# A fused attention and gated-MLP kernel on one core: the whole instruction order replaced, wv loaded ahead of the gate weights

## The chip, the cores and the metric

The kernel runs on one core of a Trainium2 chip. The metric is the device time of one execution in microseconds; lower is better. A core has a matrix engine (TensorE, PE in the profile; its weight loads are PEld), a vector engine (VectorE, DVE), an activation engine (ScalarE, ACT), a general engine (GpSimd, POOL) and a queue engine (SyncE, SP) that here does nothing but issue DMA transfers. Every engine works through its own list of instructions in order; between engines there are semaphores.

## The reference

Two branches read the same x (2048 tokens of 512 numbers, bf16) and are mixed by a gate per token. Branch A is attention with a compressive memory over 4 segments of 512 tokens, 32 heads of 16; branch B is a gated MLP with 1792 hidden features.

```python
g = sigmoid((x * gate_w).sum(-1, keepdims=True))
# A: q, k, v = x @ wq, x @ wk, x @ wv, in 32 heads of 16 and 4 segments of 512 tokens
for s in range(4):
    p = softmax(qs @ ks.T * scale + causal mask)
    a_dot = p @ vs
    a_mem = (phi(qs) @ M) / (phi(qs) @ z + 1e-6)      # phi(t) = t + 1 if t > 0 else exp(t)
    o = sigmoid(beta) * a_mem + (1 - sigmoid(beta)) * a_dot
    M, z = M + phi(ks).T @ vs, z + phi(ks).sum()
a = o @ wo
# B
b = (relu(x @ W_gate) * (x @ W_up)) @ W_down
out = g * a + (1 - g) * b
```

## The kernel before

All weights and the work of one segment lie in SBUF. `program` lists every operation of the whole computation once (1515 of them), each with what it reads and writes, and nothing in that list says when it runs. `Sched` then takes, for each of the five engines, a list of operation numbers from the table `ORDER`, walks the five lists and puts in the waits that the reads and writes call for. So the table alone decides in which order the engines work, and for a few operations which engine does them: the ReLU, the copies of q, k and v out of PSUM, the masking of k (`kp`) and the scaling of the output tile may stand in ACT's list or in DVE's. A second table, `BANKS`, gives for each accumulation the PSUM bank, of which there are eight; a matmul that begins in a bank waits until the engine that emptied it last is done. The tables were found by a search off the chip, with a planner's durations for each operation and with landing times for the first loads (`LAND0`, `DCOST`).

What PE does, by line of the code:
- L508: matmuls of ones at the start, of no use to the result. L520, L529: the first 512 tokens of x, loaded as hT, are transposed into xT by the identity; DVE and ACT copy the result (L513). Later chunks of x come transposed by DMA (L456).
- L591, L589: projections. q and k are made with features on the partitions (L591, weights wq, wk as the stationary side), v with tokens on the partitions (L589, wv as the moving side, so each of its matmuls needs one piece of wv whole: two matmuls in one operation take pieces 0 and 1, the next operation 2 and 3). The first segment's q is made in single steps, the first one in 384 and 128 columns.
- L706: attention scores, in visits of four to fourteen matmuls that use 32 rows of the array each. ACT turns them into exponentials (L717) and POOL zeroes the masked part (L726).
- L756: probabilities times values, 64 matmuls for each group of 8 heads, from vaug and from vsh, a copy of vaug shifted by 64 partitions that a DMA makes (L667). A column of vaug (L537, `vone`) makes the softmax's sums. DVE transposes, divides and transposes back (L764 to L779).
- L631, L648: the memory M and the read from it.
- L844: gate and up matmuls (wg, wu); ReLU (L852 on ACT, L853 on DVE), then the product with up (L855 on DVE) into hT.
- L881, L874: the output, seven pairs of matmuls over the hidden features (wd) and four over the heads (wo) into one bank; then a scaling by 1 - g into osb (L889 on DVE, L890 on ACT) and a store (L892). The last tile is made in two pieces of 384 and 128 columns.

Loads are issued on SP, but for hT2 (256 KB, 256 tokens of x), the first piece of wq and three tiny ones, which ACT issues (L452 for all). Each weight comes in pieces: wq, wk, wv in four of 128 KB, wg and wu in eight of 224 KB, wd in seven of 256 KB. gwb is the gate's weight spread over the partitions. ACT also loads its table at the first activation (L461).

The score visits, the L756 groups and the full matmuls differ in the part of the array they use.

Of the kernel before, what the change touches and what calls it, by code (L numbers as in the profile page):

```python
# [26 lines left out]
BANKS = ("171630520531275446756000000000047560000111115764767560667657445465554456464777507755157600774404414613500240251657751003"  # L27
         "423366410145546576053600571667673176267001021605702356603331563046063015614701000001404666454577127755074066545726565745"
         "67451706507275244216302403520425407020000014023307526164674767547654471210567123")
ORDER = {k: [int(x) for x in v.split()] for k, v in {  # L30
    "pe": """
# [17 lines left out]
1506 1481 1490 1500 1472 1482 1501 1491 1492 1502 1507 1508 1509 1510 1511 1512""",  # L49
    "act": """  # L50
# [5 lines left out]
1362 133 1326 1300 1473 1483 1493 1503""",  # L56
    "dve": """
# [9 lines left out]
1317 1463 1457 134 1464 1318 1458 1374 1366 1367 1368 1375 1376 1369 1370 1377 1371 1378 1372 1379 1380 1513""",  # L67
    "pool": """
# [331 lines left out]
def build_kernel(nc, A_x, A_wq, A_wk, A_wv, A_wo, A_beta, W_g, W_u, W_d, gate_w, out):  # L400
# [4 lines left out]
    EPS, SCALE = 1e-6, 16 ** -0.5  # L405
    sc = Sched(ORDER, BANKS)
    T = {}
# [539 lines left out]
```

## Time and profile before

| | us |
|---|---|
| median of 3 runs | 265.52 |
| the runs | 263.29, 265.52, 265.70 |
| the profiled execution | 263.63 |
| its span, first to last instruction | 262.4 |
| PE busy | 258.1 |
| ACT busy | 186.7 |
| DVE busy | 171.8 |
| POOL busy | 120.5 |

The profile shows one execution. A row of a group has the line of the code, engine and operation, what is written and read (`out<-in`), the shape, the number; then the total busy time in us and the mean of one in ns; then the idle time of the engine ahead of it and what ended most of that. A row of the order in time begins with the start in us and the length of the (merged) group; a bracket at its end tells how long the engine was idle ahead and for whom. `PEq`, `SPq`, `ACTq` are the queues that issue instructions. The records of matmuls overlap: a matmul of 512 columns is on record for 0.38 us, while the next one may start 0.216 us after it.

### The profile page before, as it was taken

Reading aid. Unit: us, or ns where it says so; the run is one execution under the profiler, and the core shown is the slowest. Engines: PE = TensorE matmul, PEld = TensorE weight load, DVE = VectorE, ACT = ScalarE, POOL = GpSimd, SP = SyncE. Lnnn points to the kernel's source line nnn. Section 1 sums busy time; section 2 is a strip of 40 time slices with the busy share of each in tenths; the row PEclk is TensorE's granted clock in tenths of the full one; section 3 lists DMA queues with packets and bytes.
Section 4 is the critical chain, followed back from the end, with each engine's and each line's share of the span. In section 5 each row is a group of like instructions: output and inputs, shape, how many; then the busy total and the mean of one; then the engine's idle time right before and its main releaser. Section 6 shows DMA issues by size and latency. Waiting matters only on the chain.

```text
span 262.4 us, 6451 instructions
## 1 busy us (share of the span) xinstructions
PE 258.1 (98%) x2655; PEld 116.4 (44%) x2655; DVE 171.8 (65%) x348; ACT 186.7 (71%) x179; POOL 120.5 (46%) x295
## 2 busy tenths in 40 slices
PE   8999999999999999999999999999999999999997
PEld 5333434444544445434544444444444445433553
DVE  2366777868867657987666716887766248866670
ACT  4579877877678855889666788887878855887103
POOL 2000586787052492466740458418734781148300
PEclk9999999999999999999999999999999999999999
DMA  7999984004205141030270300221030305200002
GB/s 213 263 307 203 298 170 140 25 3 120 45 3 124 27 117 23 2 80 1 63 128 20 81 4 0 80 45 40 2 65 1 83 3 83 42 2 0 2 2 80
DMA packets 34925, 19.61 MB, mean 75 GB/s; under 512 B 24144, under 2 KB 34256, under 8 KB 34896
## 3 DMA queue, kind: packets, MB, share of 16 engines
q1 hardware_dynamic: 34512, 18.80, 30.2%
q8 instruction: 21, 0.34, 0.6%
q10 hardware_dynamic: 384, 0.40, 0.5%
q14 instruction: 8, 0.07, 0.1%
HBM read 10.14 MB, written 2.11 MB: 47 GB/s over the span
## 4 chain that ended last, share of the span: by engine, by line
PE 94%; SPq 2%; DMA 2%; DVE 0%; issue 0%
PE ps L844 38%; PE ps L881 19%; PE ps L591 9%; PE ps L706 9%; PE ps L756 7%; PE ps L589 5%; PE ps L874 5%; SPq L452 2%; DMA wv<-in_A_wv_dram 2%; PE ps L648 1%; PE ps L631 1%; DVE rl L853 0%; DVE osb L889 0%
## 5 line engine op out<-in xcount | busy, mean ns | idle before, releaser
L717 ACT ACTIVATE E<-ps 128x2048 bf16<-128x2048 f32 (+2 forms) x87 | 135.3, 1582 | 32.8 <-PE ps L706 32.3
L726 POOL TENSOR_SCALAR_AFFINE_SELECT E<-E 64x256 bf16<-64x256 bf16 (+1 forms) x256 | 99.6, 419 | 100.2 <-ACT E L717 89.8
L844 PE MATMUL ps<-xT,wu 128*128 128x512 bf16 x224 | 60.5, 380 | 0.2 <-DVE rl L853 0.2
L844 PE MATMUL ps<-xT,wg 128*128 128x512 bf16 x224 | 59.9, 380 | 0.0
L881 PE MATMUL ps<-wd,hT 128*128 128x512 bf16 (+2 forms) x238 | 56.2, 367 | 0.0
L855 DVE TENSOR_TENSOR hT<-ps,rl 128x512 bf16<-128x512 f32 x56 | 38.1, 687 | 22.8 <-PE ps L844 22.3
L881 PEld LDWEIGHTS ps<-wd,hT 128*128 128x128 bf16 x238 | 21.4, 98 | 24.8 <-issue 2.8
L844 PEld LDWEIGHTS ps<-xT,wg 128*128 128x128 bf16 x224 | 20.6, 98 | 24.9 <-issue 1.9
L844 PEld LDWEIGHTS ps<-xT,wu 128*128 128x128 bf16 x224 | 19.9, 98 | 25.8 <-issue 3.4
L706 PE MATMUL ps<-qT,kp 32*128 32x320 bf16 (+7 forms) x512 | 27.6, 286 | 0.0
L853 DVE TENSOR_SCALAR rl<-ps 128x512 bf16<-128x512 f32 x28 | 19.2, 685 | 10.9 <-PE ps L844 10.7
L764 DVE STREAM_TRANSPOSE Tn<-ps 128x512 f32<-128x512 f32 x32 | 20.9, 693 | 6.4 <-PE ps L756 6.3
L852 ACT ACTIVATE rl<-ps 128x512 bf16<-128x512 f32 x28 | 16.5, 596 | 9.8 <-PE ps L844 9.8
L773 POOL TENSOR_TENSOR adT<-Tn,rdg 128x512 bf16<-128x512 f32 x12 | 13.1, 1095 | 20.4 <-DVE rdg L771 8.8
L706 PEld LDWEIGHTS ps<-qT,kp 32*128 32x128 bf16 x512 | 9.1, 92 | 24.2 <-ACT E L717 8.1
L589 PE MATMUL ps<-wv,xT 128*128 128x512 bf16 x64 | 17.4, 380 | 1.1 <-DMA wv<-in_A_wv_dram 1.1
L756 PE MATMUL ps<-E,vaug 64*17 64x128 bf16 (+7 forms) x512 | 18.2, 283 | 0.0
L756 PE MATMUL ps<-E,vsh 64*17 64x128 bf16 (+7 forms) x512 | 17.8, 283 | 0.0
L591 PE MATMUL ps<-xT,wk 128*128 128x512 bf16 x64 | 17.8, 380 | 0.0
L591 PE MATMUL ps<-xT,wq 128*128 128x512 bf16 (+2 forms) x68 | 17.6, 377 | 0.0
L889 DVE TENSOR_SCALAR osb<-ps,omg 128x512 bf16<-128x512 f32 (+1 forms) x10 | 7.1, 710 | 15.6 <-PE ps L874 15.6
L890 ACT ACTIVATE osb<-ps,omg 128x512 bf16<-128x512 f32 (+1 forms) x7 | 4.7, 672 | 16.5 <-PE ps L874 16.0
(70 smaller groups left out, 230.7 us busy)
## 6 DMA issues: line engine op xcount, KB each, us to landing
vsh<-vaug SPq DMA_DIRECT2D x8, 272.0 KB, 3.3
out_dram<-osb SPq DMA_DIRECT2D x15, 128.0 KB, 1.9
wg<-in_B_W_gate_dram SPq DMA_DIRECT2D x8, 224.0 KB, 5.5
wu<-in_B_W_up_dram SPq DMA_DIRECT2D x8, 224.0 KB, 5.6
osb<-in_A_x_dram SPq DMA_DIRECT2D x14, 128.0 KB, 2.2
wd<-in_B_W_down_dram SPq DMA_DIRECT2D x7, 256.0 KB, 3.6
wk<-in_A_wk_dram SPq DMA_DIRECT2D x4, 128.0 KB, 3.3
wv<-in_A_wv_dram SPq DMA_DIRECT2D x4, 128.0 KB, 3.7
```

The lines of the kernel that those rows point to most:

```text
L589: ins = e.matmul(A(ep)[:, :], lhsT=V.xT[:, kt, tok + col * 128:tok + (col + 1) * 128], rhs=w[:, kt, :], start=(kt == 0), stop=(kt == KT - 1))
L591: ins = e.matmul(A(ep)[:, c0:c1], lhsT=w[:, kt, col * 128:(col + 1) * 128], rhs=V.xT[:, kt, tok + c0:tok + c1], start=(kt == 0 and c0 == 0 ...
L706: ins = q.matmul(PS[:, ep.bank + i, o:o + w], lhsT=V.kp[r, kslot(s, G), c, :], rhs=V.qT[r, qslot(s, G), q0:q0 + w], start=True, stop=True, ...
L717: return a.activation(V.E[:, n * 512:(n + k) * 512].rearrange("q (b n) -> q b n", n=512), PS[:, x.bank:x.bank + k, :], ACT.Exp, scale=SCALE)
L726: pool(lambda g, ap=ap, lim=lim: g.affine_select(out=ap, in_=ap, compare_op=ALU.is_ge, fill=0.0, base=lim, pattern=[[0, 4], [1, 64]], chan ...
L756: ins = q.matmul(A(eps[p])[32 * jj:32 * jj + 17, 64 * (c + u):64 * (c + u + n)], lhsT=v[:, 8 * G + 2 * jj + p, :], rhs=V.E[r, f:f + 64 * n ...
L764: dve(lambda e, p=p, ep=eps[p]: e.transpose(V.Tn[:, 2 * (G % (TNN // 2)) + p, :], A(ep)[:, :]), 709, writes=[f"Tn{2 * (G % (TNN // 2)) + p ...
L844: ins = e.matmul(A(ep)[:, :], lhsT=w[:, kt, f * 128:(f + 1) * 128], rhs=V.xT[:, kt, c % XR * 512:(c % XR + 1) * 512], start=(kt == 0), sto ...
L852: sc.add(Op([("act", lambda e, ep=eg, r=r: e.activation(V.rl[:, r, :], A(ep)[:, :], ACT.Relu), t_act(512)), ("dve", lambda e, ep=eg, r=r: ...
L853: ("dve", lambda e, ep=eg, r=r: e.tensor_scalar(V.rl[:, r, :], A(ep)[:, :], 0.0, None, ALU.max), t_dve(512))],
L855: dve(lambda e, ep=eu, r=r, hs=hs: e.tensor_tensor(V.hT[:, hs, :], A(ep)[:, :], V.rl[:, r, :], ALU.mult), t_dve(512), reads=[f"rl{r}"], wr ...
L881: ins = e.matmul(A(ep)[:, 0:c1 - c0], lhsT=V.hT[:, slots[f], i * 128:(i + 1) * 128], rhs=V.wd[:, f, c0:c1], start=st_ and f == f0, stop=sp ...
```

## The change

The tables `ORDER` and `BANKS` are replaced; no other line differs, and the operations are the same ones. Two lines of each show the kind of edit:

```diff
     "act": """
-6 7 3 68 76 70 80 0 1 2 142 153 180 156 159 204 199 234 395 389 210 401 196 216 202 228 81 93 222 186 240 327 246 252 419 256 280 286 331 292 332
...
+3 6 7 68 70 76 80 0 1 2 153 142 145 156 169 159 204 193 234 389 210 199 216 401 228 93 81 407 222 240 186 246 419 252 256 449 280 286 335 292 336
...
     "sp": """
-4 5 8 9 10 11 12 13 14 15 17 18 27 20 19 16 24 21 22 90 26 23 39 25 32 88 31 38 50 28 40 98 163 37 30 29 162 35 49 33 47 34 96 45 36 208 207 44 42
...
+4 5 8 9 10 11 12 13 14 15 16 17 18 27 20 19 21 24 22 23 90 26 39 25 88 32 28 31 38 50 40 98 163 37 30 29 162 47 43 35 33 42 100 34 36 208 96 46 207
```

Operations 15 to 18 are the four pieces of wv, 19 to 26 the first halves of wg and wu, 27 is gwb; on ACT 3 is the table load with its first activation, 6 the load of hT2 and 7 that of wq. All five lists differ nearly everywhere behind the start. PE has 685 rows of equal instructions in place of 704. ACT does more of the work that either engine can do: ReLUs 31 in place of 28, copies of q 9 for 8, of k 6 for 4, of v 7 for 9, maskings of k 13 for 9, scalings of the output 8 for 6.

First place, the start. SP's loads of weights, before:

```order
L452 DMA wk<-in_A_wk_dram 128x512 x4
L452 DMA wv<-in_A_wv_dram 128x512 x3
L452 DMA gwb<-in_gate_w_dram 128x512
L452 DMA wg<-in_B_W_gate_dram 128x896 x2
L452 DMA wv<-in_A_wv_dram 128x512
L452 DMA wu<-in_B_W_up_dram 128x896
L452 DMA wg<-in_B_W_gate_dram 128x896 x2
```

and now:

```order
L452 DMA wk<-in_A_wk_dram 128x512 x4
L452 DMA wv<-in_A_wv_dram 128x512 x4
L452 DMA gwb<-in_gate_w_dram 128x512
L452 DMA wg<-in_B_W_gate_dram 128x896 x3
L452 DMA wu<-in_B_W_up_dram 128x896
L452 DMA wg<-in_B_W_gate_dram 128x896
L452 DMA wu<-in_B_W_up_dram 128x896
```

The fourth issued piece of wv moves up past gwb and two pieces of wg. PE at the same time, from the end of wq on, before:

```order
L591 MATMUL ps<-xT,wk 128x512 x2
L591 MATMUL ps<-xT,wq 128x512
L591 MATMUL ps<-xT,wk 128x512 x10
L591 MATMUL ps<-xT,wq 128x512
L706 MATMUL ps<-qT,kp 128x512 x4
L589 MATMUL ps<-wv,xT 128x512 x2
L591 MATMUL ps<-xT,wk 128x512 x2
L589 MATMUL ps<-wv,xT 128x512 x6
L844 MATMUL ps<-xT,wg 128x512 x2
```

and now:

```order
L591 MATMUL ps<-xT,wq 128x512 x12
L591 MATMUL ps<-xT,wk 128x512 x8
L589 MATMUL ps<-wv,xT 128x512 x2
L591 MATMUL ps<-xT,wk 128x512 x2
L589 MATMUL ps<-wv,xT 128x512 x2
L591 MATMUL ps<-xT,wk 128x512 x4
L706 MATMUL ps<-qT,kp 128x512 x4
L591 MATMUL ps<-xT,wk 128x512 x2
L589 MATMUL ps<-wv,xT 128x512 x6
L844 MATMUL ps<-xT,wg 128x512 x2
```

Value matmuls now begin ahead of the first scores. Second place, PE where the third segment's first output tiles are made (two tiles' worth of L874, four matmuls each; in brackets the semaphores that a row waits for), before:

```order
L874 MATMUL ps<-wo,oT 128x512 [waits s_dve]
L874 MATMUL ps<-wo,oT 128x512 x7
L844 MATMUL ps<-xT,wg 128x512 [waits s_act]
L844 MATMUL ps<-xT,wg 128x512 x3
L706 MATMUL ps<-qT,kp 128x256 [waits s_dve]
L706 MATMUL ps<-qT,kp 128x256 x7
L706 MATMUL ps<-qT,kp 128x320 [waits s_act,s_dve]
L706 MATMUL ps<-qT,kp 128x448 x2
L706 MATMUL ps<-qT,kp 128x192
L706 MATMUL ps<-qT,kp 128x64 x2
L844 MATMUL ps<-xT,wu 128x512 [waits s_dve]
L844 MATMUL ps<-xT,wu 128x512 x3
```

and now:

```order
L874 MATMUL ps<-wo,oT 128x512 [waits s_dve]
L874 MATMUL ps<-wo,oT 128x512 x7
L706 MATMUL ps<-qT,kp 128x256 [waits s_dve,s_act]
L706 MATMUL ps<-qT,kp 128x256 x7
L706 MATMUL ps<-qT,kp 128x320
L706 MATMUL ps<-qT,kp 128x448 x2
L706 MATMUL ps<-qT,kp 128x192
L706 MATMUL ps<-qT,kp 128x64 x2
L881 MATMUL ps<-wd,hT 128x512 [waits s_dve]
L881 MATMUL ps<-wd,hT 128x512 x3
```

The gate matmuls between the output and the scores are gone, and a further output tile begins right behind the scores; its wait for DVE is for L889 of the second tile. Third place, PE's end, before:

```order
L874 MATMUL ps<-wo,oT 128x512 x7
L881 MATMUL ps<-wd,hT 128x384 x2
L881 MATMUL ps<-wd,hT 128x512 x2
L874 MATMUL ps<-wo,oT 128x512 x4
L874 MATMUL ps<-wo,oT 128x384 x4
L881 MATMUL ps<-wd,hT 128x128 x10
L874 MATMUL ps<-wo,oT 128x128 x4
```

and now:

```order
L874 MATMUL ps<-wo,oT 128x512 x7
L881 MATMUL ps<-wd,hT 128x384 x2
L874 MATMUL ps<-wo,oT 128x512 x4
L881 MATMUL ps<-wd,hT 128x128 x2
L874 MATMUL ps<-wo,oT 128x128 x4
L881 MATMUL ps<-wd,hT 128x384 x2
L874 MATMUL ps<-wo,oT 128x384 x4
```

The two pieces of the last tile change places, so that the wider one is finished last; its scaling stands in ACT's list, that of the narrow one in DVE's.

More of the change, by code (lines that the diff above doesn't have):

```diff
@@ L26 @@
 CORDER = [[(0, 1, 7, 2, 6, 3, 5, 4), (4, 1, 7, 2, 6, 3, 5, 0)] * 2] * 4
-BANKS = ("171630520531275446756000000000047560000111115764767560667657445465554456464777507755157600774404414613500240251657751003"
-         "423366410145546576053600571667673176267001021605702356603331563046063015614701000001404666454577127755074066545726565745"
-         "67451706507275244216302403520425407020000014023307526164674767547654471210567123")
+BANKS = ("701342567041527367060111111000076674000000017746406641677557057660745455757454564555067547054561100243156300254312024440"
+         "000032601066124506725713302304356764655776571765057551202160263063036006466400000011667175542704477063043464664775757676"
+         "57661705075020500150260213503516547013213213546076745462767225760667057651602741")
 ORDER = {k: [int(x) for x in v.split()] for k, v in {
     "pe": """
[17 rows of a table removed]
-1506 1481 1490 1500 1472 1482 1501 1491 1492 1502 1507 1508 1509 1510 1511 1512""",
-    "act": """
[5 rows of a table removed]
-1362 133 1326 1300 1473 1483 1493 1503""",
-    "dve": """
[9 rows of a table removed]
-1317 1463 1457 134 1464 1318 1458 1374 1366 1367 1368 1375 1376 1369 1370 1377 1371 1378 1372 1379 1380 1513""",
-    "pool": """
[8 rows of a table removed]
-1364 1322 1358 1346 1329 1327 1340 1330 1360 1301 1302 1328 1324""",
[17 rows of a table added]
+1508 1509 1510 1471 1498 1481 1499 1472 1492 1500 1482 1511 1512 1501 1502""",
+    "act": """
[5 rows of a table added]
+1320 1344 1415 1332 1421 1350 1338 1439 1356 1433 1362 1326 1300 1457 1473 1503""",
+    "dve": """
[9 rows of a table added]
+1318 1368 1376 1369 1377 1370 1371 1372 1378 1379 1380 1493 1483 1513""",
+    "pool": """
[8 rows of a table added]
+1354 1358 1322 1352 1363 1327 1329 1364 1348 1328 1330 1301 1302""",
     "sp": """
[3 rows of a table removed]
-1484 1494 1504 1514""",
[3 rows of a table added]
+1494 1484 1514 1504""",
 }.items()}
```

80 rows, old and new, of the table ORDER are left out of this document.

## The prediction

> **What bounds the kernel now.** I read the page first, then the waits of TensorE (PE), then the start, the places of the waits and the end in order of time. From the page:
>
> ```profile
> span 262.4 us, 6451 instructions
> PE 258.1 (98%) x2655; PEld 116.4 (44%) x2655; DVE 171.8 (65%) x348; ACT 186.7 (71%) x179; POOL 120.5 (46%) x295
> ...
> PE 94%; SPq 2%; DMA 2%; DVE 0%; issue 0%
> ```
>
> PE (the first column of the busy line) is busy for 98% of the span and carries 94% of the chain that ended last. A new order can then win only three things: time in which PE stands still, the price of switching between kinds of matmul, and the two ends of the program. The longest of PE's waits (total us, times, longest):
>
> ```profile
> PE ps L589 <- DMA wv<-in_A_wv_dram: 1.1, 1, 1.1
> ...
> PE ps L844 <- DVE rl L853: 0.2, 1, 0.2
> ```
>
> One wait stands out, the one for a piece of wv. (The line left out is the launch, which no order moves.) Busy time alone hides part of a wait, because a matmul's record overlaps the next one's; so I take the pace of the starts as the measure. In the first fence below are pieces of the chain (start, length, what, how many), in the second rows in order of time:
>
> ```profile
> 72.72 0.55 PE ps L706 x14
> 94.14 2.59 PE ps L844 x12
> 186.12 1.10 PE ps L756 x64
> 128.50 2.14 PE ps L756 x127
> ```
>
> ```profile
> 24.48 0.59 PE L844 MATMUL ps<-xT,wu 128*128 128x512 bf16 x2
> 25.01 0.40 PE L706 MATMUL ps<-qT,kp 32*128 32x256 bf16 x8
> 25.34 0.60 PE L844 MATMUL ps<-xT,wu 128*128 128x512 bf16 x2
> ```
>
> Twelve full matmuls take 2.59 us, 0.216 each. After the two that start at 24.48 the next would start at 24.91; the scores start at 25.01, so leaving the full matmuls costs 0.10. Eight score matmuls (the step at L706) then hold PE for 0.33, fourteen for 0.55. Two neighbouring groups of L756 take 2.14 together, two lone ones 2 x 1.10, so putting them side by side saves 0.06.
>
> **The wait for wv (removed).** The start in order of time:
>
> ```profile
> 0.80 0.40 ACTq L452 DMA_DIRECT2D hT<-in_A_x_dram  x1
> 1.74 1.28 ACT L461 ACT_TABLE_LOAD   x1 [1.74 <-PEq L932]
> 3.03 0.21 ACT L461 ACTIVATE eb<-const-bfloat16-1.0 128x8 f32<-128x8 bf16 x1
> 4.13 0.85 PE L529 MATMUL ps<-ident,hT 128*128 128x128 bf16 x6
> 5.04 1.38 SPq L452 DMA_DIRECT2D wv<-in_A_wv_dram  x3
> 5.97 0.38 ACT L513 ACTIVATE xT<-ps 128x256 bf16<-128x256 f32 x1 [0.36 <-PE ps L529]
> 5.98 0.37 ACTq L452 DMA_DIRECT2D adT<-in_B_W_gate_dram  x1
> 7.89 0.43 SPq L452 DMA_DIRECT2D wv<-in_A_wv_dram  x1
> ...
> 12.14 0.40 PE L706 MATMUL ps<-qT,kp 32*128 32x512 bf16 x4
> 13.67 0.60 PE L589 MATMUL ps<-wv,xT 128*128 128x512 bf16 x2 [1.13 <-DMA wv<-in_A_wv_dram]
> ```
>
> Four score matmuls from 12.14 would hand over at about 12.14 + 0.33 = 12.47; the value matmuls start at 13.67. The wait costs 1.20 us. Its cause is the place of one 128 KB load on SP, issued at 7.89 behind gwb and two wg pieces:
>
> ```profile
> DMA to landing us min/median/max: 3.1/3.7/5.7
> ...
> hT<-in_A_x_dram ACTq DMA_DIRECT2D x1, 256.0 KB, 3.0
> out_dram<-osb SPq DMA_DIRECT2D x1, 96.0 KB, 1.6
> out_dram<-osb SPq DMA_DIRECT2D x1, 32.0 KB, 1.4
> ```
>
> (first row: the four pieces of wv). In the new order all four are issued one after another, so the fourth at about 5.04 + 3 x 0.475 = 6.5. With the median of 3.7 it lands at 10.2, with the worst of 5.7 at 12.2. In the old order the scores at 12.14 stand behind the transposes of x, 20 matmuls of wq and 12 of wk. In the new one the second pair of wv, the first to need the last two pieces, stands behind the transposes and as many matmuls: 20 of wq, 10 of wk, 2 of wv. So PE comes to it at 12.14 less the switch, 12.0, and to the first pair four matmuls earlier, at 11.2. At the median the wait is gone with 1.8 to spare, at the worst 0.2 is left: -1.20, bounds -1.20 and -1.0. The two wg pieces that stood ahead of that wv piece now stand behind it. They land about when it did, at 7.89 + 5.7 = 13.6, and their first matmul comes 14 matmuls and one visit of scores behind that pair, at 12.0 + 3.0 + 0.4 = 15.4. I cost this at nothing; what hides it is that margin of 1.8.
>
> **The small waits of the old order (-0.51).** Two more places are off the pace:
>
> ```profile
> 104.83 0.60 PE L844 MATMUL ps<-xT,wg 128*128 128x512 bf16 x2
> 105.46 0.43 PE L648 MATMUL ps<-Mbd,phiq 128*128 128x136 bf16 x4
> 143.15 1.03 PE L874 MATMUL ps<-wo,oT 128*128 128x512 bf16 x4
> 144.22 0.75 DVE L889 TENSOR_SCALAR osb<-ps,omg 128x512 bf16<-128x512 f32 x1 [0.28 <-PE ps L874]
> 144.97 0.62 PE L706 MATMUL ps<-qT,kp 32*128 32x256 bf16 x14
> 145.83 1.04 PE L844 MATMUL ps<-xT,wu 128*128 128x512 bf16 x4 [0.24 <-DVE rl L853]
> ```
>
> 104.83 + 2 x 0.216 = 105.26, but L648 starts at 105.46: 0.20, with no record of what it waited for. 144.97 + 0.55 = 145.52, but L844 starts at 145.83: 0.31, behind the ReLU on DVE. Both places are written anew, so both terms go.
>
> **A new wait at the third segment's boundary (+0.35).** In the new order the eight L874 matmuls are followed at once by the 14 score matmuls and then by L881 that waits for DVE: for the scaling at L889 of the tile that L874 has just finished. By the rows above: the last of four L874 starts at 143.80, DVE begins at 144.22, 0.42 later, and takes 0.75. With 0.05 for the signal (an estimate: 144.22 less 143.15 + 1.03, the end of the group) L881 is free 1.22 after the start of that matmul. PE gets there at pace after 0.216 + 0.10 + 0.55 = 0.87. So it waits 0.35; bounds 0 (if DVE's part is one of two waits and the other scaling, on ACT, is what it needs) and 0.75, a whole scaling.
>
> **Switches and groups (-0.26).** Full matmuls are left 61 times instead of 63: 2 x 0.10. The groups of L756 stand in 11 stretches instead of 12: 0.06. The number of matmuls of each kind is the same.
>
> **The end (+0.42).** The last tile's two column pieces change places: the 384 columns come last and go to ACT, where the 128 came last and went to DVE.
>
> ```profile
> L890 ACT ACTIVATE osb<-ps,omg 128x384 bf16<-128x384 f32 x1 | 0.6, 581 | 0.0
> L889 DVE TENSOR_SCALAR osb<-ps,omg 128x128 bf16<-128x128 f32 x1 | 0.3, 350 | 6.2 <-PE ps L874 6.2
> ```
>
> The scaling grows by 0.581 - 0.350 = 0.23, the store from 1.4 to 1.6 (its rows are above), 0.19 unrounded. Nothing lies beside them. 0 to 0.5.
>
> **Work moved from DVE to ACT (0).** By the counts of the two orders ACT gains 3 ReLUs, 3 copies of q or k, 4 maskings of k and 2 scalings, and loses 2 copies of v.
>
> ```profile
> L852 ACT ACTIVATE rl<-ps 128x512 bf16<-128x512 f32 x28 | 16.5, 596 | 9.8 <-PE ps L844 9.8
> L611 ACT ACTIVATE kp<-kT,pm 128x512 bf16<-128x512 bf16 x9 | 6.4, 716 | 0.0
> 150.00:247.00 97.00, 97.00 (x1081) 43.18 (x1087) 61.95 (x123) 73.10 (x67) 52.89 (x128) 1.00 0.15 31
> ```
>
> Taking a copy for as long as a ReLU, that is 4 x 0.596 net, 4 x 0.716, and 2 scalings at DVE's 0.75: 6.8 us. Between 150 and 247 us, in the last row, ACT is busy for 73.1 (the figure with x67) of 97: 24 us of idle in two fifths of the program cover it. Without that cover 6.8 is the upper bound; nothing on the path is the lower, and I take it, since a moved piece only costs where an exponential queues behind it.
>
> **Sum.** -1.20 - 0.51 - 0.26 + 0.35 + 0.42 = -1.2 us. The profiled execution took 263.63 us (its span and 1.2 around it), so one like it would take 262.4. It is 1.9 below the median of the three runs (263.29, 265.52, 265.70); the mean of all four is 264.5. I set the change on that mean: 263.3 us.
>
> [...]
>
> **Rivals.**
> *The table load holds hT back.* ACT now begins with the table load and its activation, ahead of the loads of hT (256 KB) and wq. If ACT issued them only when both are done, hT would be issued at 0.80 + 1.28 + 0.21 = 2.3 instead of 0.80, land 3.0 later at 5.3, and PE, which needs it at 4.13, would stand for 1.2: 263.6 like the profiled, 264.5 on the mean. Against it: at 5.98 ACT issues a load 0.01 after it began a copy of 0.38, so an issue does not wait for the work ahead. It costs something from a delay of 0.3 on.
> [...]
> *ACT becomes the bound, and the kernel slower.* Should 1.2 of the moved 6.8 us fall where the exponentials already hold PE, the gain is gone; with all of it the time is 263.3 + 6.8 = 270.1, and with 4.9 (268.2 less 263.3) it is over 1% slower than the median. For it: PE has no slack to give, and every score visit waits for an exponential. Against it: the idle time above.
> *The change does not take the wait away.* The value matmuls need their bank freed by a copy of q on ACT too. If that copy is what ends last, the 1.2 stays in another name: 264.5. Against it: the first pair comes 8 matmuls, 1.7 us, behind the last of wq, and a copy takes 0.6.
> *A late load elsewhere.* The shifted copy vsh is issued behind the ones column of v, which stands later in the new DVE order.
>
> ```profile
> 28.94 1.17 SPq L667 DMA_DIRECT2D vsh<-vaug  x2
> 40.21 1.10 PE ps L756 x64
> DMA to landing us min/median/max: 2.9/3.3/6.9
> ```
>
> Its halves are issued at 28.94 and 29.5; with the worst 6.9 the second is there at 36.4, 3.8 us ahead of the first L756. The new DVE order has the ones column behind the second chunk's first copy of k; I put that 3 us later, and SP has a wd piece between the halves: second half near 33. With 6.9 it lands at 39.9, against a first L756 1.2 earlier than before, at 39.0: 0.9 lost, 264.2. With the median 3.3 it has 2.7 to spare.
>
> **How the numbers follow.** The sum as worked out: 0.66, 263.3. Table load 0.07, 264.5. Wait kept under another name 0.07, 264.5. Late loads 0.12, 264.2. ACT bound 0.08, 264.5 to 270.1, over 1% slower for the last third. One per cent of 265.52 is what a measurement of this kernel can tell from no change, so faster means under 262.9. The runs reach 1.2 to either side of their mean; a median of three lies nearer. Of the first case I take 0.4 below 262.9, which gives 0.26; slower (over 268.2) gets 0.06: 0.03 of ACT's case, and 0.03 for what I did not see; within 1% 0.68. The range: down to 261.7, where the new waits come to nothing (0.35 and 0.42 less) and the runs are low; up to 265.7, which takes in all rivals but ACT's far end.
>
> **What would show it.** No wait of PE for wv at 11 to 14 us; PE's first L529 still at 4.1 and ACT's issue of hT at 0.8 (right) or 2.3 (table load); a wait of 0.35 at L881 behind L889 near 143; L890 with 384 columns as the last instruction, the end 0.4 later after PE's last matmul. Wrong would be a PE whose waits add up to over 1.5 us, or a row of L717 ahead of PE's waits in many places.

## The result and the profile after

| | before | after |
|---|---|---|
| median of 6 runs, us | 264.56 | 261.62 |
| lowest and highest | 263.29, 265.70 | 261.20, 262.41 |
| the profiled execution | 263.63 | 261.58 |
| its span | 262.36 | 260.35 |

After to before: 0.9895, with a 95% interval from 0.9854 to 0.9936. The changed kernel is about 1% faster, and its runs lie closer together. The page of the changed kernel (span; busy time, share and number of each engine; shares of the chain that ended last):

```profile
span 260.3 us, 6440 instructions
PE 256.8 (99%) x2655; PEld 115.8 (44%) x2655; DVE 168.4 (65%) x338; ACT 191.3 (73%) x189; POOL 119.7 (46%) x295
...
PE 91%; SPq 3%; DMA 2%; DVE 1%; issue 1%; ACT 0%
```

PE does the same 2655 matmuls and is still the bound. ACT has 4.6 us more to do and DVE 3.4 less. The waits of PE (total, times, longest), changed kernel:

```profile
PE ps L508 <- PEq L932: 0.8, 1, 0.8
PE ps L881 <- DVE osb L889: 0.3, 1, 0.3
```

The wait for wv is not among them; besides the launch there is one, which is new. The start of the changed kernel in order of time (start, length, engine, line):

```profile
0.80 1.28 ACT L461 ACT_TABLE_LOAD   x1 [0.80 <-PEq L932]
0.86 0.39 ACTq L452 DMA_DIRECT2D hT<-in_A_x_dram  x1
...
3.93 0.50 PE L529 MATMUL ps<-ident,hT 128*128 128x128 bf16 x4
4.45 0.40 PE L520 MATMUL ps<-ident,hT 128*128 128x128 bf16 x4
4.68 0.39 PE L529 MATMUL ps<-ident,hT 128*128 128x128 bf16 x4
4.93 3.62 PE L591 MATMUL ps<-xT,wq 128*128 128x384 bf16 x20
...
10.12 0.59 PE L589 MATMUL ps<-wv,xT 128*128 128x512 bf16 x2
...
10.98 0.59 PE L589 MATMUL ps<-wv,xT 128*128 128x512 bf16 x2
...
14.44 0.59 PE L844 MATMUL ps<-xT,wg 128*128 128x512 bf16 x2
```

Two things are to be seen. ACT's load of hT is issued at 0.86, inside the table load that lasts from 0.80 to 2.08: ACT's new beginning holds nothing back. And the four transposes from 4.45 take 0.23 until the next begin, 0.057 each, where those of the kernel before, at 4.13, took 0.107 each by their starts. Here the record of full clock begins at 4.18 us, in the profile of before at 6.58. PE is at its first wg matmul at 14.44 instead of 15.84, although it has four full matmuls (0.86 us) more behind it by then. So the start gave 1.40 + 0.86 = 2.26 us, not 1.20.

Around 18 us a small wait is new. DVE and PE in the changed kernel, in order of time:

```profile
16.59 0.69 DVE L551 CUSTOM_DVE_ANT_0 osb<-osb,gwb 128x512 bf16<-128x512 bf16 x1 [2.23 <-DMA osb<-in_A_x_dram]
...
17.82 0.69 DVE L575 TENSOR_TENSOR ek<-ek,ttmp 128x1024 bf16<-128x1024 bf16 x1
18.43 0.35 DVE L610 TENSOR_SCALAR kp<-kT,pm 128x512 bf16<-128x512 bf16 x1
18.69 0.68 DVE L853 TENSOR_SCALAR rl<-ps 128x512 bf16<-128x512 f32 x1
```

DVE stood 2.23 us for a tile of x (osb) whose gate reduction stands first in its list; ek, kp and a ReLU queued behind it, and PE's L844 came 0.24 off its pace at 19.43 (the pace before it, 18.98 + 0.216, from single matmuls of the trace). The third segment's boundary, changed kernel:

```profile
140.66 1.03 PE L874 MATMUL ps<-wo,oT 128*128 128x512 bf16 x4
...
141.62 0.62 PE L706 MATMUL ps<-qT,kp 32*128 32x256 bf16 x14
141.73 0.75 DVE L889 TENSOR_SCALAR osb<-ps,omg 128x512 bf16<-128x512 f32 x1 [1.11 <-PE ps L874]
...
142.53 1.04 PE L881 MATMUL ps<-wd,hT 128*128 128x512 bf16 x4 [0.30 <-DVE osb L889]
```

141.62 + 0.55 for fourteen score matmuls is 142.17; L881 begins at 142.53, 0.36 late, 0.05 behind the end of the scaling. And the end:

```profile
257.24 0.81 PE L874 MATMUL ps<-wo,oT 128*128 128x384 bf16 x4
258.09 0.58 ACT L890 ACTIVATE osb<-ps,omg 128x384 bf16<-128x384 f32 x1 [2.67 <-PE ps L874]
```

PE ends at 258.05 and the span 2.29 later; before it was 1.88 (260.48 to 262.36).

The pair adds up: wait for wv -1.20, rest of the start -1.06, two small waits -0.51, switches -0.26, the new wait +0.36, the wait at 19 us +0.24, the end +0.41: -2.02 of the -2.05 between 263.63 and 261.58. (The switches are the counted ones; no row gives them by themselves.) What the pair does not tell is whether the 1.06 belongs to the change, since the time of full rate may be chance, and why the medians are 2.9 apart. That is what the experiments were for.

### The profile page after: what moved, and what is told of

It reads as the page before. It is cut to its first block, busy times and chain, and to the rows that moved or that the text cites. A ratio compares the mean times of both kernels' runs of the same rounds, so it can differ in the third digit from the quotient of the medians.

```text
span 260.3 us, 6440 instructions
## 1 busy us (share of the span) xinstructions
PE 256.8 (99%) x2655; PEld 115.8 (44%) x2655; DVE 168.4 (65%) x338; ACT 191.3 (73%) x189; POOL 119.7 (46%) x295
## 4 chain that ended last, share of the span: by engine, by line
PE 91%; SPq 3%; DMA 2%; DVE 1%; issue 1%; ACT 0%
PE ps L844 37%; PE ps L881 19%; PE ps L706 8%; PE ps L591 8%; PE ps L756 7%; PE ps L874 5%; PE ps L589 4%; SPq L452 3%; DMA osb<-in_A_x_dram 2%; PE ps L648 1%; PE ps L631 1%; DVE osb L889 0%; DVE rl L853 0%; DVE ek L575 0%; DVE hT L551 0%
## 5 line engine op out<-in xcount | busy, mean ns | idle before, releaser
L726 POOL TENSOR_SCALAR_AFFINE_SELECT E<-E 128x256 bf16<-128x256 bf16 (+1 forms) x256 | 98.8, 417 | 107.8 <-ACT E L717 100.7
L844 PE MATMUL ps<-xT,wu 128*128 128x512 bf16 x224 | 60.0, 380 | 0.1
L844 PE MATMUL ps<-xT,wg 128*128 128x512 bf16 x224 | 59.1, 380 | 0.0
L881 PE MATMUL ps<-wd,hT 128*128 128x512 bf16 (+2 forms) x238 | 56.4, 367 | 0.3 <-DVE osb L889 0.3
L881 PEld LDWEIGHTS ps<-wd,hT 128*128 128x128 bf16 x238 | 21.4, 98 | 25.2 <-issue 2.7
L844 PEld LDWEIGHTS ps<-xT,wg 128*128 128x128 bf16 x224 | 20.6, 98 | 25.5 <-issue 2.4
L844 PEld LDWEIGHTS ps<-xT,wu 128*128 128x128 bf16 x224 | 20.3, 98 | 25.2 <-issue 3.4
L852 ACT ACTIVATE rl<-ps 128x512 bf16<-128x512 f32 x31 | 18.4, 595 | 10.6 <-PE ps L844 9.8
L853 DVE TENSOR_SCALAR rl<-ps 128x512 bf16<-128x512 f32 x25 | 17.3, 693 | 10.2 <-PE ps L844 10.0
L890 ACT ACTIVATE osb<-ps,omg 128x512 bf16<-128x512 f32 (+1 forms) x9 | 6.1, 677 | 16.2 <-PE ps L874 16.0
L591 PE MATMUL ps<-xT,wk 128*128 128x512 bf16 x64 | 17.1, 380 | 0.0
L591 PE MATMUL ps<-xT,wq 128*128 128x512 bf16 (+2 forms) x68 | 16.8, 367 | 0.0
L874 PE MATMUL ps<-wo,oT 128*128 128x512 bf16 (+2 forms) x68 | 16.2, 367 | 0.0
## 6 DMA issues: line engine op xcount, KB each, us to landing
wd<-in_B_W_down_dram SPq DMA_DIRECT2D x7, 256.0 KB, 3.7
```

The lines of the kernel that those rows point to most:

```text
L591: ins = e.matmul(A(ep)[:, c0:c1], lhsT=w[:, kt, col * 128:(col + 1) * 128], rhs=V.xT[:, kt, tok + c0:tok + c1], start=(kt == 0 and c0 == 0 ...
L726: pool(lambda g, ap=ap, lim=lim: g.affine_select(out=ap, in_=ap, compare_op=ALU.is_ge, fill=0.0, base=lim, pattern=[[0, 4], [1, 64]], chan ...
L844: ins = e.matmul(A(ep)[:, :], lhsT=w[:, kt, f * 128:(f + 1) * 128], rhs=V.xT[:, kt, c % XR * 512:(c % XR + 1) * 512], start=(kt == 0), sto ...
L852: sc.add(Op([("act", lambda e, ep=eg, r=r: e.activation(V.rl[:, r, :], A(ep)[:, :], ACT.Relu), t_act(512)), ("dve", lambda e, ep=eg, r=r: ...
L874: ins = e.matmul(A(ep)[:, 0:c1 - c0], lhsT=V.oT[:, ot[G], i * 128:(i + 1) * 128], rhs=V.wo[:, G, c0:c1], start=st_ and G == 0, stop=sp_ an ...
L881: ins = e.matmul(A(ep)[:, 0:c1 - c0], lhsT=V.hT[:, slots[f], i * 128:(i + 1) * 128], rhs=V.wd[:, f, c0:c1], start=st_ and f == f0, stop=sp ...
```

## The experiments

Ten further kernels were run, in three groups, each beside fresh runs of the kernel before on the same chip; the kernel before itself was profiled twice more.

| kernel | median us | lowest to highest (runs) | to before, 95% |
|---|---|---|---|
| before + wv1 ahead | 263.14 | 262.39 to 264.60 (12) | 0.9963, 0.9938 to 0.9988 |
| before + ACT's beginning | 264.31 | 262.78 to 266.66 (12) | 1.0013, 0.9978 to 1.0048 |
| after, ACT's older beginning | 261.89 | 261.34 to 262.49 (7) | 0.9916, 0.9883 to 0.9949 |
| before + both | 263.33 | 262.82 to 264.19 (12) | 0.9980, 0.9956 to 1.0003 |
| before + wv1 and wu ahead | 262.37 | 261.95 to 262.88 (9) | 0.9916, 0.9885 to 0.9947 |
| after, pieces at the end swapped | 261.35 | 261.13 to 262.30 (6) | 0.9883, 0.9846 to 0.9921 |
| after, ek and kp first | 261.37 | 261.15 to 262.01 (6) | 0.9877, 0.9838 to 0.9916 |
| after, both of these | 261.51 | 261.21 to 261.82 (6) | 0.9884, 0.9847 to 0.9920 |
| after, ek and kp first, the older end | 260.96 | 260.73 to 261.51 (6) | 0.9889, 0.9864 to 0.9914 |
| after, wv1 back | 265.64 | 264.39 to 267.33 (12) | 1.0046, 1.0013 to 1.0078 |

The kernel before had medians of 263.74 (30 runs, for the first four), 264.55 (14, for the next four) and 264.12 (17, for the last two): its median wanders, so a ratio of one group is not to be compared finely with one of another.

**wv ahead, alone.** Only the place of wv1 (operation 16) on SP is moved:

```diff
-4 5 8 9 10 11 12 13 14 15 17 18 27 20 19 16 24 21 22 90 26 ...
+4 5 8 9 10 11 12 13 14 15 16 17 18 27 20 19 24 21 22 90 26 ...
```

> Before, with nothing changed but SP's list: the fourth issued piece of wv moves ahead of gwb and two pieces of wg. Theory A (the sum of the prediction): the wait of 1.20 ahead of L589 goes and nothing takes its place, so 1.2 us less than before, about 263.3 on before's median of 264.56; PE's first full-rate matmul comes at any time between 4 and 7.5 us, as luck has it in each execution. Theory B (the start decides): PE still stands idle for 0.16 between its opening matmuls and the transposes, as in before, and comes to full rate late (about 6.6); the time falls by 1.2 all the same but its executions spread over 2 us as before's do. A rival for the wv step: the bank of the first L589 becomes what is waited for, and the time stays within 0.3 of before.

Measured 263.14. The wait for wv is gone and PE is at its first wg at 14.43 instead of 15.84. But later, in order of time:

```profile
33.44 0.59 PE L844 MATMUL ps<-xT,wg 128*128 128x512 bf16 x2
34.73 0.61 PE L844 MATMUL ps<-xT,wu 128*128 128x512 bf16 x2 [0.70 <-DMA wu<-in_B_W_up_dram]
```

33.44 + 2 x 0.216 = 33.87, so PE stands 0.86 for a piece of wu that landed at 34.7; in the kernel before it landed at 34.35 and was wanted at 34.86. Two shorter stops, 0.15 at 17.18 and 0.27 at 32.58, also end just behind landings of wu, at 17.13 and 32.49. The three take back 1.28 of the 1.41 us: PE is at that last piece of wu only 0.13 earlier than before, and the profiled execution is 0.11 shorter (263.52 to 263.63). The medians differ by more, 0.60, since this execution is one of the slower ones of its kernel. Moving wv up by itself is not the gain: the older order is held by its loads until 35 us.

**ACT's beginning, alone, and taken back.** In the kernel before, the table load goes ahead of the loads; in the changed kernel, back behind them:

```diff
     "act": """
-6 7 3 68 76 70 80 ...
+3 6 7 68 76 70 80 ...
```

```diff
     "act": """
-3 6 7 68 70 76 80 ...
+6 7 3 68 70 76 80 ...
```

> Before, with nothing changed but the first three entries of ACT's list: the table load and its activation ahead of the loads of hT2 and wq, as in the changed kernel. Theory A: no effect beyond 0.3 us (the first tile hT0 lands up to 0.3 earlier, since hT2 is issued 0.06 later); full rate comes when luck has it. Theory B: hT0 lands before the opening matmuls end (3.4 instead of 3.7), PE is not idle there, and full rate comes at about 4.2 in place of 6.6; half rate for 2.4 us less is 1.2 us less, with 0.28 from the earlier start about 1.0 to 1.5 us less than before, and the executions lie closer together (within 1.3 us).

> The changed kernel, with ACT's list beginning as before's does: loads of hT2 and wq first, then the table load. Theory A: within 0.3 us of the changed kernel (261.6). Theory B: hT0 lands at 3.7, PE stands idle for 0.16 between opening matmuls and transposes, full rate comes near 6.6, the time is 1.0 to 1.5 us longer (about 263) and spreads over 2 us.

Measured 264.31 and 261.89. In the old order nothing is gained: the executions at full clock have a median of 263.43, those of the kernel before beside them 263.60. In the new one the median is 0.27 higher, with spreads that overlap almost wholly (261.34 to 262.49 and 261.20 to 262.41), so no loss is shown. In the first the transposes begin at 3.36 instead of 3.73, and all of that is waited away, for wv at 13.14 and for two pieces of wu behind it, at 33.68 (0.09 behind the piece's landing, though the profile names DVE there) and at 35.66. The first and the last of these:

```profile
13.14 0.60 PE L589 MATMUL ps<-wv,xT 128*128 128x512 bf16 x2 [0.84 <-DMA wv<-in_A_wv_dram]
...
35.66 0.60 PE L844 MATMUL ps<-xT,wu 128*128 128x512 bf16 x2 [0.53 <-DMA wu<-in_B_W_up_dram]
```

The theory that the earlier start makes the gain fell with these two.

**Both in the kernel before.** The two edits above together.

> Before with both edits: wv ahead of the gate pieces on SP, table load first on ACT. Theory A: as with wv alone, 1.2 us less than before. Theory B: the two add up, 1.2 and 1.0 to 1.5, so 2.2 to 2.7 us less than before, about 262.1; the whole new order then is worth no more than some 0.5 beyond these two edits.

Measured 263.33, no better than wv alone. PE waits for two pieces of wu, 0.69 at 17.19 and 0.51 at 34.15. So each of the two theories held so far was too simple, and a third took their place: what is gained early is only kept if the loads behind it come early too, or are wanted later. In the changed kernel the last piece of wu stands behind two pieces of wd on SP instead of four: it lands at 32.39 instead of 34.35 and is first used at 35.00, about when it was before (34.86).

**wu ahead as well.** On top of the first edit, the last pieces of wu (33, 34, 36) are issued ahead of pieces of wd (49, 47, 45):

```diff
-... 29 162 35 49 33 47 34 96 45 36 208 207 ...
+... 29 162 35 33 34 36 49 47 96 45 208 207 ...
```

> The kernel before with wv1 moved ahead of gwb on SP as in the first run, and the last pieces of wu issued ahead of those of wd. Theory C (the kernel before is held to its stream of loads until about 35 us, so that what the four wv pieces give is taken back by waits for wu): the wait for wv is gone, the stall of 0.86 us in front of wu at 34.7 us is gone too, nothing near it takes its place, and the time is 262.3 to 262.6, 1.2 or more under the kernel before. Rival (the wu wait is only moved to wd or to another load behind it, or the rest is not a matter of loads): a wait of 0.5 us or more stays between 14 and 60 us, and the time is that of the first run, about 263.1.

Measured 262.37, as forecast (262.3 to 262.6). Its rows at the place of the old stall:

```profile
33.49 0.59 PE L844 MATMUL ps<-xT,wu 128*128 128x512 bf16 x2
33.92 0.59 PE L844 MATMUL ps<-xT,wg 128*128 128x512 bf16 x2
...
40.64 0.59 PE L844 MATMUL ps<-xT,wu 128*128 128x512 bf16 x2
41.58 1.04 PE L844 MATMUL ps<-xT,wg 128*128 128x512 bf16 x4 [0.35 <-DVE Tn L764]
```

No wait for wu; 0.51 of what was won is lost again at 41.58 (40.64 + 0.43 = 41.07), now behind DVE, which had stood 1.93 us for a tile of x (osb). That is the wait of 0.5 us or more that the rival named, but the time is not the rival's 263.1. Four loads issued earlier on SP, with not one instruction of PE, DVE or ACT moved, bring 0.84% by the ratio, where the whole change brings 1.05%.

**The pieces of the end swapped.** In the changed kernel the 128-column piece (1511, 1512) comes last again:

```diff
-... 1472 1492 1500 1482 1511 1512 1501 1502""",
+... 1472 1492 1500 1482 1501 1502 1511 1512""",
...
-1494 1484 1514 1504""",
+1494 1484 1504 1514""",
```

> The changed kernel with the last tile's pieces in the older order again, 128 columns last on VectorE. If the longer end costs what the rows say (2.29 us from the last matmul to the end of the span, against 1.88 before), the span ends 0.4 us earlier: 261.2. Rival (the end is set by the store's fixed latency, or PE ends later by another order of its last groups): no difference, 261.6.

Measured 261.35, but not for the reason given: from the last matmul (258.39 + 0.39) to the end of the span (261.06) it is still 2.28 us. Only six matmuls of 128 columns (0.33 us) now stand between the two pieces, and the two stores, in the row below, follow one another on SP: that of the narrow piece, whose data were ready at 259.17, was issued at 259.47, 0.38 behind the wide one.

```profile
259.09 0.81 SPq L892 DMA_DIRECT2D out_dram<-osb  x2
```

The profile is also of use for another thing. This execution came late to full rate (record of full clock from 6.49), and took 262.30:

```profile
4.51 0.61 PE L520 MATMUL ps<-ident,hT 128*128 128x128 bf16 x4
4.91 0.63 PE L529 MATMUL ps<-ident,hT 128*128 128x128 bf16 x4
5.34 4.20 PE L591 MATMUL ps<-xT,wq 128*128 128x384 bf16 x20
```

The twenty matmuls of wq take 4.0 us until the next line begins (9.37), against 3.46 above.

**ek and kp ahead of two gate reductions; and both edits.**

```diff
-... 183 158 91 92 161 174 395 ...
+... 183 158 161 174 91 92 395 ...
```

> The changed kernel with the making of ek and kp on VectorE ahead of two gate reductions. If the 0.24 us of PE at 19 us come from the ReLU that waits for kp behind the reductions that wait for osb, they go: PE runs at its pace from 18.5 to 20 us and the time is 261.35. Rival (the reductions are wanted as soon as they can be had, and what they give is late instead): a wait of the same size or a larger one stands between 19 and 36 us, 261.6 or more.

> The changed kernel with both edits, the older end and the making of ek and kp first. If the two are independent terms of the path, their gains add: 0.65 us less than the changed kernel, about 261.0, with the only wait of PE over 0.2 us left at L881 near 142. Rival (one of them is hidden by the other or taken back by a later load): between 261.2 and 261.6.

Measured 261.37 and 261.51. The wait at 19 us is gone in both profiles: from the first wg matmul to the last matmul of all it is 243.37 us in each, against 243.61 in the changed kernel. Together they do not add, since the swapped end gave nothing; the sum of 0.65 was wrong in that half. These two profiles alone do not show that the edit took the wait away: in the run before, without it, the wait was absent too, since PE came a microsecond later there, behind the reduction, and in these two PE came 0.68 and 0.33 later than in the changed kernel. The next run, with PE as early, shows it.

The profiled executions of these three kernels have records of full clock from 6.49, 5.93 and 4.83, and took 262.30, 262.01 and 261.64: 0.40 us of time for each us (0.66 for 1.66, the first against the last). Nearly all of that lies ahead of the first wg matmul, at 15.42, 15.12 and 14.76. The changed kernel with ACT's older beginning falls in line, with full clock from 5.27 and 261.78. So the new order's time follows the moment of full rate, and its spread from 261.2 to 262.4 is of that size.

**The older end whole.** With ek and kp first, and all of the narrow piece behind the wide one, as before:

```diff
-... 1480 1507 1508 1509 1510 1471 1498 1481 1499 1472 1492 1500 1482 1511 1512 1501 1502""",
+... 1480 1471 1498 1481 1499 1472 1492 1500 1482 1501 1502 1507 1508 1509 1510 1511 1512""",
```

> The changed kernel with ek and kp made first, as before, and with the end of PE as it was in the kernel before: the whole 128-column piece, ten matmuls of wd and four of wo, behind the 384-column piece. With 128 columns last but only six matmuls between the pieces the end did not move (2.28 us from the last matmul to the span's end); theory: what counts is that the two last stores are issued 0.4 us or more apart on SP, and with fourteen matmuls between them the end is 1.9 us, 0.4 us less. Time about 261.0, and from the start of the first wg group to the last matmul 243.4 us as in the three runs before. Rival (the 384-column piece, wanted 0.56 us earlier, waits for the down projection's input): a wait of PE over 0.2 us between 250 and 257 us and no gain.

Measured 260.96, the lowest of all kernels. Its end:

```profile
256.79 0.72 PE L881 MATMUL ps<-wd,hT 128*128 128x128 bf16 x10
256.99 0.58 ACT L890 ACTIVATE osb<-ps,omg 128x384 bf16<-128x384 f32 x1 [2.34 <-PE ps L874]
257.35 0.39 PE L874 MATMUL ps<-wo,oT 128*128 128x128 bf16 x4
257.77 0.35 DVE L889 TENSOR_SCALAR osb<-ps,omg 128x128 bf16<-128x128 f32 x1 [1.00 <-PE ps L874]
```

1.89 us from the last matmul (257.74) to the end (259.63), and 243.39 from the first wg to it, with PE as early (14.34) as in the changed kernel and the gate reduction on DVE no earlier (16.65, there 16.59): so it is the edit that takes the wait at 19 us away. Both terms came as forecast, 0.66 us under the changed kernel's median by a sum of 0.65. The two were not timed side by side. Of the 0.38 by which the end is shorter than with the pieces merely swapped, 0.27 is the later issue of the narrow store there, and the rest its longer way from issue to landing behind the wide one (1.57 to 1.46 here).

**wv1 back in the changed kernel.**

```diff
-4 5 8 9 10 11 12 13 14 15 16 17 18 27 20 19 21 24 ...
+4 5 8 9 10 11 12 13 14 15 17 18 27 20 19 16 21 24 ...
```

> The changed kernel with wv1 back behind gwb and the first wg pieces on SP. Theory C (the kernel before was held to the loads until 35 us; the new order is not): PE waits for wv1, which lands near 13.6 us, at the first or second group that multiplies by wv, between 10 and 13.6 us, 1.2 to 2.5 us in all, and no load behind it gives this back, so that the time is 1.2 us or more above the changed kernel: 262.8 to 264. Rival (the new body order hides it, so the move of wv1 itself is worth nothing in it): under 262.2.

Measured 265.64, 4.0 us over the changed kernel and more than any theory had. Of its waits the first:

```profile
PE ps L589 <- DMA wv<-in_A_wv_dram: 3.1, 1, 3.1
```

The new order wants wv at 10.3, so the same landing at 13.6 costs 3.29 us of pace instead of 1.20. The rest of the loss stands just behind that wait. Order of time, and a table by stretch (from:to, length, busy time of PE, PEld, DVE, ACT and POOL with their numbers, granted clock, share of DMA, GB/s):

```profile
13.60 0.60 PE L589 MATMUL ps<-wv,xT 128*128 128x512 bf16 x2 [3.12 <-DMA wv<-in_A_wv_dram]
14.04 0.86 PE L591 MATMUL ps<-xT,wk 128*128 128x512 bf16 x2
14.69 1.06 PE L589 MATMUL ps<-wv,xT 128*128 128x512 bf16 x2
15.55 1.91 PE L591 MATMUL ps<-xT,wk 128*128 128x512 bf16 x4
```

```profile
10.00:14.20 4.20, 1.08 (x6) 0.31 (x4) 0.61 (x2) 2.52 (x4) 0.00 (x0) 1.00 0.93 321
14.20:17.60 3.40, 3.40 (x13) 1.02 (x10) 1.81 (x4) 0.00 (x0) 0.00 (x0) 0.50 1.19 268
```

From 14.23 to 17.65 us the granted clock (third figure from the end) is 0.50, and matmuls start 0.43 apart instead of 0.216. The record: full clock from 3.99 for 10.24 us, half for 3.41, then full. So PE lost its clock for 3.41 us here, from 0.63 behind the end of the wait on, and with starts 0.43 apart for 0.216 that costs half of it, 1.7 us. Over this program that is a mean granted clock of 1 - 1.7 / 265.2 = 0.994, and each execution's mean clock is on record: six of this kernel's twelve are at 0.994, with a median of 266.66, against 264.67 for the six at 1.000. So the 4.0 us is a mixture: 3.05 over the changed kernel without the loss of clock, which is about the wait, and 5.04 with it.

**Two further profiles of the kernel before.**

> The kernel before once more, for a second profiled execution beside that of 263.63 us. Theory C: its time follows the landing of its loads; an execution at 265 or above shows wv1 or wu landing later than 13.62 and 34.35 us, by about the difference, and longer waits of PE for them; what follows 36 us has the same length. Rival: the difference lies in when PE comes to its full rate (6.58 us in the first), or behind 36 us.

> As the run before it, for a third profiled execution of the kernel before: the same two theories, by the landings of wv1 and wu, the waits for them, the time of the full rate and the length of the rest behind 36 us.

263.40 and 263.21 us, both at full clock, so neither shows an execution above 265. But the two, first fence and second, and the first profile with its 13.67 and 263.63, tell what sets the time at full clock:

```profile
12.05 0.40 PE L706 MATMUL ps<-qT,kp 32*128 32x512 bf16 x4
13.45 0.61 PE L589 MATMUL ps<-wv,xT 128*128 128x512 bf16 x2 [1.00 <-DMA wv<-in_A_wv_dram]
```

```profile
11.32 0.39 PE L706 MATMUL ps<-qT,kp 32*128 32x512 bf16 x4
13.26 0.60 PE L589 MATMUL ps<-wv,xT 128*128 128x512 bf16 x2 [1.55 <-DMA wv<-in_A_wv_dram]
```

PE reached its scores at 12.14, 12.05 and 11.32, 0.8 us apart. That did not matter: the wv matmuls began with the landing of wv1, at 13.67, 13.45 and 13.26, and the times are 263.63, 263.40 and 263.21, each the start of the wv matmuls plus 249.95 or 249.96. Coming to the scores earlier only makes the wait longer, 1.61 us off pace in the last (11.32 + 0.33 to 13.26).

**All executions by granted clock.** Of the 61 timed ones of the kernel before in the three groups, 46 are at 1.000 with a median of 263.66 and 15 at 0.994 with one of 265.65. With ACT's beginning moved, which leaves the wait for wv and lets PE reach it earlier, 5 of 12 are at 0.994. Of the eight other kernels of the table and the changed one, in whose profiles PE does not wait for wv at 10 to 14 us, not one of 70 is. So in these counts the second group appears only with the wait for wv. That the clock falls just behind it in the kernel before as it does in the changed one with wv1 back, was not seen, since no profile of before is at 0.994: it rests on this count and on the size (1.7 us for one such stretch; 2.0 between the medians).

## Why the prediction was right or wrong

It gave 263.3 us, 261.7 to 265.7; the time is 261.62. The direction and most terms hold; the point is 1.7 us too high and the range just misses. 261.62 is under the line of 262.9 that the prediction drew for "faster", to which it gave 0.26; at 1.05% below the kernel before, with an interval of 0.6 to 1.5%, it is not clear of "within 1%" (0.68). As a change, -1.2 was forecast, the pair shows -2.05 and the medians -2.94. The executions of before that were timed in the experiments and are at full clock have a median of 263.66, 2.04 above the changed kernel, as the pair has it; the other 0.9 is there because three of before's six runs lie above 265.

- *The wait for wv, -1.20.* The mechanism was right, and its size is what failed. The 1.20 was read from one execution whose full rate came late. In the three profiles of before the wait is 1.07, 1.20 and 1.61 off pace: PE came to the scores anywhere from 11.32 to 12.14, and the landing, at 13.26 to 13.67, did not follow it. With the wait gone, PE keeps what an earlier full rate gives: the pair differs by 2.26 at the first wg. The term of the sum that reads "the wait costs 1.20" should have been "PE is set free of the landing": 1.2 where full rate comes late, and 1.06 more in the execution that was profiled. Two figures bear this out. In the profile whose full clock came at 6.49, nearly as late as before's 6.58, the first wg is at 15.42, which is 0.42 and the four matmuls' 0.86 better, 1.28 in all. And 0.40 for each of the 2.40 us between 6.58 and 4.18 is 0.96 of the 1.06.
- *The setting on the mean of four executions.* "One like it would take 262.4" came out well: the profiled executions of the changed body that came late to full rate took 262.01 (record from 5.93) and 262.30 (6.49). A little of that is luck, for the 0.24 at 19 us, which the sum lacks, is missing in these two. The next step, adding 0.9 since the mean of four was 264.5, was wrong. It takes the spread of before for something that both kernels share. The runs above 265 in it (two of the four) belong, by their size, to the second group, and that group goes with the wait; the changed kernel has none in its six. What a later full rate adds to the spread, the runs show: 0.40 us per us in the new order (the 0.66 for 1.66 above), and in the old one, at full clock, nothing but another length of the wait (1.07 to 1.61 off pace).
- *The loads behind it, costed at nothing.* Right for the changed kernel, whose wg is not waited for: the two pieces landed at 13.28 and 13.90, and the first matmul is at 14.44. But the sum treated the wv move as a term that stands alone. In the older order it gives 0.60 between the medians and 0.11 between the profiled executions, because wu is late at 17.1, 32.5 and 34.7; in the new one, taken back, it costs 4.0. The new order's other part is that the last piece of wu lands 1.96 earlier, and 2.6 ahead of its use; the prediction has no term for that.
- *Two small waits, -0.51, and switches, -0.26.* No wait is left at either place, and the sum of the pair closes to 0.03 with them.
- *The new wait at the third segment's boundary, +0.35.* 0.36, at L881 behind L889, at 142.5.
- *The end, +0.42.* 0.41. The size was right and the reason half so: with 128 columns last and six matmuls between, it is as long; with fourteen it is 0.40 shorter. What counts is that the narrow store need not wait on SP behind the wide one (issued 0.38 apart with six matmuls between, 0.55 with fourteen).
- *Not foreseen: +0.24 at 19 us,* the gate reduction that waits for osb at the head of DVE's list. It shows when PE is early.
- *The table load as a rival* fell: hT is issued at 0.86, inside it, and PE's first L529 is at 3.93. What stands behind the load is ACT's first activation, at 2.09, just after the load's end at 2.08. *ACT as the bound* fell: 191.3 us of work, and no wait of PE for an exponential. *Wait under another name* and *late vsh* did not come.

## What to carry to other kernels

The wait for wv's landing hid everything ahead of it (PE came to the scores from 11.32 to 12.14, and the time did not follow), so its length in one profile, 1.20, is not what its removal gave, 2.26 at the first wg: ask when the engine would have been there in other executions, and which load is needed next; the gain lasted only as far as the following loads allowed (waits for wu took back 1.28 of 1.41 us in the older order). When runs of a kernel fall in two groups, look at each one's granted clock before averaging them: in the profile with wv1 back a wait of PE cost its 3.29 us and then 1.7 us of lost clock. And when a wide and a narrow store end a program, ask whether the second can be issued as soon as its data are ready; which of them is last did not decide here (2.29 us from PE's end with the wide one last, 2.28 with the narrow one).

## What the runs showed of the hardware

- With wv1 back, PE waited 3.12 us, to 13.60; the granted clock was 0.50 from 14.23 to 17.65, 3.41 us, though PE was busy through all of them, and full again behind. Behind the end of PE's work in the changed kernel the clock falls too, at 260.18, when PE has been idle for 2.13 us (since 258.05). The stretch of full clock ahead of the fall lasts 10.24 us in the first profile and 256.0 in the second. What sets the moment of a fall, the runs do not tell.
- Two kernels whose profiles show waits of PE of up to 0.86 us, at 17 and at 34 us (before + wv1 ahead, before + both), have a mean clock of 1.000 in all of their 24 executions.
- The record of full clock begins anywhere from 3.69 to 6.58 us in the profiles that have one, with PE's first matmul at 0.84 to 0.85 in each; none shows the 7.5 us that the first expectation allows.
- A DMA issue on ACT's queue goes on during the table load: 0.86, with the load from 0.80 to 2.08. ACT's piece of hT then landed at 3.80 to 3.96, as with the older beginning (3.78 to 3.88). The first piece of hT, which SP issues at 0.81 in either order, landed at 3.15 to 3.40 instead of 3.56 to 3.71. Why, the runs do not tell.
- Two stores that were ready for issue on SP's queue were issued 0.38 us apart: 257.56 and 257.93 in the changed kernel, 259.09 and 259.47 with its pieces swapped, where the second one's data were ready at 259.17.
